# Packed attention and a gated feed-forward block on one core: another table of steps up to the first remainder

## The chip, the cores and the metric

The kernel runs on one core of a Trainium2 chip. Its engines work side by side, each through its own list of instructions in order: TensorE (PE) multiplies, with its weight loads shown apart as PEld; VectorE (DVE) and ScalarE (ACT) do the elementwise work; GpSimd (POOL) helps with a few additions; SyncE (SP) issues the transfers. Where one engine needs what another makes, it waits on a semaphore. The metric is the time of one execution on the device in microseconds (us), as the median of several runs.

## The reference, cut to what matters

```python
def sm_attn(qq, kk, vv):
    s = scale * np.matmul(qq, kk.transpose(0, 1, 3, 2))
    s = s - np.max(s, axis=-1, keepdims=True)
    a = np.exp(s)
    a = a / (np.sum(a, axis=-1, keepdims=True) + 1e-09)
    return np.matmul(a, vv)
p_packed = sm_attn(p, k, v)
out = sm_attn(q, p_packed, p_packed)
...
h = x @ w_in
g = h * (1.0 / (1.0 + np.exp(-h)))
return (g @ w_out).astype(np.float32)
```

There are 8 batches, 8 heads of 64, 576 tokens a batch and 32 packed queries a head; x is the attention's output with the heads side by side (4608 x 512), w_in is 512 x 2048 and w_out 2048 x 512. All inputs are float32.

## The kernel before, in words

The tokens of a batch come in two halves of 288, of which 256 go through the main path; the 32 left over of each half ("rest") are gathered and go through the second product later, four such groups for two batches. The feed-forward block is cut into 16 slices of 128 hidden columns. A unit is one batch and one slice. For each unit PE makes the hidden values (`h_products`, L489: 12 products, 6 a half), ACT takes Silu of them twice, once as float32 and once rounded (`h_values`, L507 to L509), DVE makes the rounding's remainder (`h_lower`, L514), and PE multiplies with the second weight (`out_products`, L521: upper and lower parts, three products for each of four token blocks).

The attention's second half and the first weight are merged: "packs" are the packed values times w_in, four slices at a time (`Packs`: products at L211, split into upper and lower parts at L458 and L461), so that a unit's hidden values are the shares of a token (a2) times a pack.

The weights arrive as 64-bit integers and are turned into float32 on the chip, in 20 chunks: fetched (`wf`, a DMA), scaled by ACT (`ws`, L179 and L180), signed by DVE (`wz`, L184 and L185), joined (`wj`, L191 and L192; for w_out the addition is POOL's), and for w_out split into upper and lower parts (`wu` on ACT, L200, `wl` on DVE, L204). Chunks 0 to 7 are one slice each, even ones of w_in and odd ones of w_out; chunks 8 to 19 are two slices each. Some chunks are staged in a pool of two buffers, some in places of `win` that are not yet in use; a fetch into a place waits until its last chunk is done with.

Up to the first rest group nothing is scheduled by a rule: a table (`ORDER`) names steps one after the other, and each step writes its instructions into the lists of the engines that it uses. So the table sets the order on PE, DVE, ACT and SP at once. In the names, `k`, `q`, `v` load a batch's inputs; `a` and a letter is a step of the attention of batch b: `as` first scores, `ac` their copies, `am` largest, `ax` exponentials, `ar` reciprocals, `at` turned, `ay` spread (16 small DMAs for batches 1 and up, L288), `aa` packed values, `an`, `ai`, `aj` scaled, turned and copied, `aS` second scores, `aC` and `aB` copied and turned to tokens (batch 0 alone), `aT` turned, `aM` less the largest, `aX` exponentials, `aD` shares, `aU` turned back (batch 0 alone), `aH` and `aL` upper and lower part of the shares. `h`, `g`, `l`, `o` and a number are the four steps of a unit, with .0 and .1 where they are done by halves; `pp`, `pu`, `pl` a pack's three; `e` rows of the result; `b` reads partial sums back. `W` and a number is `keep_warm`: as many products of a unit matrix, whose result nobody reads, which keep PE busy.

Units 0 to 3 are batch 0's first slices, 4 to 7 its next; 8 to 15 are batch 1's; 16 to 23 batch 0 again, 24 to 31 batch 1 again; unit 32 is the first rest group. Behind the table a loop runs over the other units and writes the steps of the next batch between them (`step_of`); its first act is `packs_in(2, 1, 2)`, two packs of batch 2.

PE's results go to two pools of two buffers each: `ps_acc` for sums over slices and batch 0's attention, `ps_two` for everything else. A buffer is taken in turn, so a step that takes one waits until the last user but one of that pool has been read. Inputs (`kvq_t`) share two buffers in the same way.

Of the kernel before, what the change touches and what calls it, by code (L numbers as in the profile page):

```python
# [19 lines left out]
P = 128  # L20
# [28 lines left out]


ORDER = """
k0 wf0 ws0 as0.0 as0.1 wf1 am0.0 wf2 am0.1 ax0.0 v0 ax0.1 wz0 W5 at0.0 ay0.0 ar0 W2 wf3 q0 ws2 wj0 ws1 at0.1
W1 wf4 wf5 W5 ay0.1 wz1 aa0 wz2 W2 wj1 an0 ai0 aj0 pp0 aS0.0 ws3 wz3 aS0.1 wu1 wl1 W1 aC0.0 aC0.1 pu0 ws5
aB0.0 wj3 aB0.1 wj2 pl0 aM0.0 wf6 k1 aM0.1 aX0.0 wu3 aD0.0 wf7 W18 ws4 aU0.0 v1 aX0.1 as1.0 aH0.0 aD0.1 W2
aU0.1 wz4 ws6 wl3 ac1.0 as1.1 W5 wj4 ws7 aH0.1 ac1.1 pp1 am1 pu1 wf8 aL0.0 pp2 pl1 pu2 pl2 ax1.0 aL0.1 ax1.1
h0.0 g0.0 at1.0 at1.1 h0.1 wz6 q1 wf9 h1.0 l0.0 wj6 o0.0 g0.1 h1.1 l0.1 wz7 o0.1 ws8 wz5 g1.0 l1.0 pp3 wj5
g1.1 wj7 h2.0 l1.1 pu3 wu5 wz8 ay1 pl3 o1.0 g2.0 wl5 o1.1 wu7 h2.1 ws9 l2.0 wl7 ar1 wf10 wj8 wf11 g2.1 o2.0
h3.0 l2.1 wz9 aa1 g3.0 l3.0 o2.1 ws10 an1 ai1 h3.1 wj9 o3.0 aj1 g3.1 wz10 aS1.0 pp4 aT1.0 aS1.1 pu4 l3.1
wj10 ws11 o3.1 wu10 pl4 h4 g4 aT1.1 h5 aM1.1 wl10 l4 wz11 h6 aM1.0 g5 v2 aX1.1 aX1.0 wj11 o4 l5 g6 h7 aD1.0
o5 wu11 l6 wl11 g7 pp5 o6 aD1.1 k2 pu5 l7 wf12 aH1.0 ws12 wf13 as2.0 aH1.1 aL1.0 o7 pl5 aL1.1 ac2.0 e7.1  # L60
as2.1 ac2.1 am2 ws13 h8 e7.0 g8 h9 l8 g9 h10 pp6 wz12 wz13 ax2.0 l9 o8 ax2.1 wj12 wj13 pu6 wf14 g10 l10 o9
ws14 pl6 h11 at2.0 at2.1 g11 wf15 ar2 ws15 l11 wz14 wj14 o10 h12 g12 wz15 l12 o11 wj15 wu14 h13 o12 g13 wf16
l13 h14 wu15 wl15 ay2 o13 wl14 ws16 g14 h15 wz16 l14 o14 wj16 g15 wf17 l15 ws17 pp7 pu7 wf18 pl7 o15 aa2 h16
e15.0 e15.1 an2 h17 ws18 g16 wz17 wz18 h18 q2 l16 g17 o16 ai2 l17 wj17 aj2 o17 g18 pp8 pu8 aS2.0 wj18 l18
wf19 o18 pl8 h19 b0 aT2.0 ws19 h20 g19 aM2.0 wu18 h21 l19 g20 o19 k3 h22 l20 g21 wl18 wz19 o20 aS2.1 wj19
l21 wu19 g22 o21 aT2.1 l22 wl19 h23 o22 aX2.0 pp10 aD2.0 g23 pp9 pu10 l23 pu9 pl10 o23 pl9 e23.1 h24 h25 g24
e23.0 aH2.0 l24 b1 g25 h26 l25 aM2.1 h27 o24 g26 l26 o25 g27 l27 h28 o26 g28 o27 aX2.1 l28 h29 g29 o28 l29
h30 o29 v3 aD2.1 g30 h31 l30 o30 aH2.1 aL2.1 g31 g32 aL2.0 l31 pp11 l32 pu11 pl11 o31 e31.1 e31.0
"""


# [11 lines left out]
def packed_attention_ffn(ctx: ExitStack, tc: tile.TileContext, pkT, qT, vA, vB, w_in, w_out, out):  # L83
# [13 lines left out]
    nc = tc.nc  # L97
# [29 lines left out]

    def keep_warm(n):

        ps = two_banks()  # L130
        for _ in range(n):
            nc.tensor.matmul(ps[:, 0, :P], ident, ident, start=True, stop=True)
# [83 lines left out]
    class Attention:  # L216
# [80 lines left out]
        def packed(self):  # L297
            v = made["v", self.b]
            self.ps = two_banks()[:, 0] if self.b else sum_banks()[:, 0]
            for par in range(2):  # L300
                for c in range(5):
                    n = min(P, S - c * P)
                    for i in range(NI):
                        h = 2 * i + par
                        if self.b:
                            e = self.e1T[:n, c, i, NP * par : NP * par + NP]
                        else:
                            e = self.e1T[:n, par, c, NP * i : NP * i + NP]
                        nc.tensor.matmul(  # L309
                            self.ps[NP * i : NP * i + NP, par * D : par * D + D],  # L310
                            e,
                            v[:n, c, h * D : h * D + D],
                            start=(c == 0),
                            stop=(c == 4),
                        )
# [258 lines left out]
    def load_parts(b):  # L574
# [171 lines left out]
```

## Time and profile before

| | us |
|---|---|
| median of 3 runs (lowest, highest) | 713.01 (712.46, 713.09) |
| span of the profiled execution, first to last instruction | 711.0 |
| PE busy in it | 692.0 |
| DVE busy | 336.7 |
| ACT busy | 326.7 |
| POOL busy | 18.0 |
| granted clock of PE, mean | 0.996 |
| products of `keep_warm` (L132) | 82 rows, 12.4 us |
| hidden products (L489) | 1536 rows, 454.4 us |
| second products (L521) | 1728 rows, 679.9 us |

Products overlap, so the sums of L489 and L521 are larger than the time that they take together; a row of PE's is not its time from start to start. The timeline lists instructions by start and duration with the idle time before them and what ended it; `x36` behind a row is that many in a run. One product of `keep_warm` makes two rows, and so does each other product of float32. The view by stretches gives the busy time of each engine in a window. The chain of waits goes back from the last instruction to what each one waited for. Line numbers are those of the kernel before; in the changed one all lines from L131 on are one higher.

### The profile page before, as it was taken

How to read it: one execution, taken by the hardware profiler on the slowest of the kernel's cores; microseconds unless marked ns; L12 is line 12 of the kernel's file. 1: busy time of each engine (PE TensorE's matmuls, PEld its weight loads, DVE VectorE, ACT ScalarE, POOL GpSimd, SP SyncE). 2: the span in 40 equal slices, each digit the busy share in tenths (PEclk: the TensorE clock that was granted, in tenths of full speed). 3: DMA queues.
4: the chain of work that ended last, by engine and by line, in shares of the span. 5: the costliest groups of instructions: out<-in, count | busy, mean ns of one | idle time of the engine just before them, and what ended most of it. 6: DMA issues, size and time to landing. Idle time of an engine off the chain costs nothing.

```text
span 711.0 us, 12198 instructions
## 1 busy us (share of the span) xinstructions
PE 692.0 (97%) x5098; PEld 567.0 (80%) x5098; DVE 336.7 (47%) x506; ACT 326.7 (46%) x614; POOL 18.0 (3%) x16
## 2 busy tenths in 40 slices
PE   6789999999999999999999999999999999999997
PEld 4567787878878888888878888878878788888886
DVE  4899997665353336331552315533362333622112
ACT  4577887554434426362532625453352532533221
POOL 0011111110000000000000000000000000000000
PEclk9999999999999999999999999999999999999999
DMA  9858255705012130312111121021301210010002
GB/s 327 322 168 349 76 185 183 265 1 185 1 60 82 33 139 1 111 33 87 67 60 61 39 88 67 27 100 36 137 1 59 83 35 1 1 60 1 0 1 74
DMA packets 31509, 64.15 MB, mean 90 GB/s; under 512 B 19424, under 2 KB 19424, under 8 KB 27104
## 3 DMA queue, kind: packets, MB, share of 16 engines
q1 hardware_dynamic: 31360, 63.26, 25.5%
q8 instruction: 40, 0.66, 0.4%
q10 hardware_dynamic: 96, 0.13, 0.1%
q14 instruction: 13, 0.11, 0.0%
HBM read 47.71 MB, written 11.53 MB: 83 GB/s over the span
## 4 chain that ended last, share of the span: by engine, by line
PE 89%; DVE 6%; DMA 2%; issue 1%; ACT 1%; SPq 0%; DVEq 0%; ACTq 0%
PE ps_acc L521 54%; PE ps_two L489 27%; PE ps_two L211 6%; DMA kvq_t<-in_qT 2%; PE ps_two L309 1%; DVE g_lo L514 1%; DMA kvq_t<-in_pkT 1%; DVE wo_lo L204 1%; DVE win L185 1%; DVE win L191 1%; DVE win L184 0%; DVE win L192 0%; PE ps_acc L211 0%; DVE pw_lo L461 0%; DVE w_raw L184 0%
## 5 line engine op out<-in xcount | busy, mean ns | idle before, releaser
L521 PE MATMUL ps_acc<-wo_hi,g_hi 128*128 128x512 f32 x576 | 229.2, 398 | 0.0
L521 PE MATMUL ps_acc<-wo_lo,g_hi 128*128 128x512 f32 x576 | 225.4, 391 | 0.8 <-DVE wo_lo L204 0.8
L521 PE MATMUL ps_acc<-wo_hi,g_lo 128*128 128x512 f32 x576 | 225.3, 391 | 0.0
L514 DVE TENSOR_TENSOR g_lo<-g,g_hi 128x512 fp32r<-128x512 f32 (+1 forms) x132 | 90.8, 688 | 261.3 <-ACT g_hi L508 261.3
L507 ACT ACTIVATE g<-ps_two 128x512 f32<-128x512 f32 (+1 forms) x132 | 77.5, 587 | 271.2 <-PE ps_two L489 245.6
L489 PE MATMUL ps_two<-a_hi,pw_hi 128*128 128x288 f32 x512 | 152.3, 298 | 2.6 <-DVE pw_lo L461 1.7
L489 PE MATMUL ps_two<-a_lo,pw_hi 128*128 128x288 f32 x512 | 151.5, 296 | 0.0
L489 PE MATMUL ps_two<-a_hi,pw_lo 128*128 128x288 f32 x512 | 150.6, 294 | 0.0
L521 PEld LDWEIGHTS ps_acc<-wo_hi,g_hi 128*128 128x128 f32 x576 | 108.0, 188 | 40.2 <-issue 19.1
L521 PEld LDWEIGHTS ps_acc<-wo_hi,g_lo 128*128 128x128 f32 x576 | 108.1, 188 | 24.4 <-DVE g_lo L514 0.8
L521 PEld LDWEIGHTS ps_acc<-wo_lo,g_hi 128*128 128x128 f32 x576 | 108.2, 188 | 19.6 <-DVE wo_lo L204 1.5
L489 PEld LDWEIGHTS ps_two<-a_hi,pw_hi 128*128 128x128 f32 x512 | 96.4, 188 | 8.1 <-DVE pw_lo L461 2.0
L489 PEld LDWEIGHTS ps_two<-a_lo,pw_hi 128*128 128x128 f32 x512 | 96.1, 188 | 3.5
L489 PEld LDWEIGHTS ps_two<-a_hi,pw_lo 128*128 128x128 f32 x512 | 96.2, 188 | 0.0
L508 ACT ACTIVATE g_hi<-ps_two 128x512 fp32r<-128x512 f32 (+1 forms) x132 | 76.7, 581 | 7.3 <-PE ps_acc L521 7.3
L461 DVE TENSOR_TENSOR pw_lo<-ps_two,pw_hi 128x1024 fp32r<-128x1024 f32 (+1 forms) x35 | 38.3, 1126 | 15.0 <-ACT pw_hi L458 15.0
L458 ACT CAST pw_hi<-ps_two 128x1024 fp32r<-128x1024 f32 (+1 forms) x35 | 31.6, 943 | 21.9 <-PE ps_two L211 21.9
L211 PE MATMUL ps_two<-win,ppT 64*32 64x512 f32 (+1 forms) x560 | 32.5, 560 | 0.4 <-DVE ppT L332 0.4
L509 ACT ACTIVATE rest<-ps_two 128x64 f32<-128x64 f32 (+1 forms) x132 | 30.5, 231 | 0.0
L507 ACT ACT_TABLE_LOAD x15 | 19.2, 1283 | 0.7 <-DVE g_lo L514 0.6
L211 PEld LDWEIGHTS ps_two<-win,ppT 64*32 64x32 f32 x560 | 8.0, 105 | 14.2 <-issue 10.9
L179 ACT ACTIVATE w_raw<-w_raw 128x1024 int32<-128x1024 uint32 (+1 forms) x13 | 13.3, 1021 | 9.5 <-DMA w_raw<-in_w_in 6.2
(101 smaller groups left out, 445.5 us busy)
## 6 DMA issues: line engine op xcount, KB each, us to landing
kvq_t<-in_pkT SPq DMA_DIRECT2D x7, 1216.0 KB, 5.4
kvq_t<-in_vA SPq DMA_DIRECT2D x8, 1024.0 KB, 6.9
out<-o SPq DMA_DIRECT2D x16, 512.0 KB, 2.9
kvq_t<-in_qT SPq DMA_DIRECT2D x7, 1152.0 KB, 5.1
w_raw<-in_w_in SPq DMA_DIRECT2D x6, 1024.0 KB, 8.4
win<-in_w_out SPq DMA_DIRECT2D x3, 1024.0 KB, 6.5
w_raw<-in_w_out SPq DMA_DIRECT2D x3, 1024.0 KB, 4.9
tm<-tm SPq DMA_DIRECT2D x56, 40.0 KB, 2.0
```

What stands on the lines that cost most here:

```text
L179: nc.scalar.activation(low, low.bitcast(U32), AF.Copy, scale=2.0**-29)
L185: nc.vector.scalar_tensor_tensor(low, up, -(2**31), low, op0=ALU.bitwise_and, op1=ALU.bitwise_or)
L191: nc.vector.tensor_scalar(z, up, 3, None, op0=ALU.logical_shift_left)
L211: nc.tensor.matmul(bank(par)[NP * i : NP * i + NP], lhs(r, i), rhs(r, i), start=True, stop=True)
L458: nc.scalar.copy(self.hi, self.ps[:, :, : self.nf * P])
L461: nc.vector.tensor_tensor(self.lo, self.ps[:, :, : self.nf * P], self.hi.bitcast(F32), ALU.subtract)
L489: nc.tensor.matmul(bank, p[:, par, cols], a[:, par], start=(n == 0), stop=(n == len(todo) - 1))
L507: nc.scalar.activation(g, ps[..., :MAIN], AF.Silu)
L508: nc.scalar.activation(g_hi, ps[..., :MAIN], AF.Silu)
L509: nc.scalar.activation(to, ps[..., MAIN:HS], AF.Silu)
L514: nc.vector.tensor_tensor(g_lo[:, c], g[:, c], g_hi[:, c].bitcast(F32), ALU.subtract)
L521: nc.tensor.matmul(bank, g[:, rows], w[:, f], start=(first and n == 0), stop=(last and n == 2))
```

## The change

The table of steps is another one, with the same steps except for the `W`s: 69 products of them, in 8 places, instead of 41 in 9. `keep_warm` now holds one tile for as long as no other step takes a buffer of `ps_two`, instead of taking one at each call. Nothing behind the table is changed.

```diff
 ORDER = """
-k0 wf0 ws0 as0.0 as0.1 wf1 am0.0 wf2 am0.1 ax0.0 v0 ax0.1 wz0 W5 at0.0 ay0.0 ar0 W2 wf3 q0 ws2 wj0 ws1 at0.1
+W8 wf0 wf1 ws0 wz0 wj0 ws1 k0 as0.0 wz1 wj1 W2 as0.1 am0.0 am0.1 wf2 wu1 wl1 ax0.0 W10 at0.0 v0 wf3 ay0.0 ax0.1 q0
...
     def two_banks():
 
+        made.pop("warm", None)
         return ps_two.tile([P, 2, 512], F32, name="ps_two")
...
     def keep_warm(n):
 
-        ps = two_banks()
+        if "warm" not in made:
+            made["warm"] = two_banks()
         for _ in range(n):
-            nc.tensor.matmul(ps[:, 0, :P], ident, ident, start=True, stop=True)
+            nc.tensor.matmul(made["warm"][:, 0, :P], ident, ident, start=True, stop=True)
```

On PE, around the second half of batch 0's attention, the list was this. L211 into `ps_acc` are the second scores (`aS0`), L359 the turns to tokens (`aB0`), L132 the fillers, L379 and L381 the turns back (`aU0`):

```order
L211 MATMUL ps_acc<-kvq_t,ppT 32x288 x16
L132 MATMUL ps_two<-ident 128x128
L359 MATMUL ps_acc<-ident,tm 128x128 x10
L132 MATMUL ps_two<-ident 128x128 x18
L379 MATMUL ps_acc<-ident,tm 128x128 x2
L381 MATMUL ps_acc<-ident,tm 128x32
```

Now the same place on PE reads:

```order
L212 MATMUL ps_acc<-kvq_t,ppT 32x288 x8
L133 MATMUL ps_two<-ident 128x128 x4
L360 MATMUL ps_acc<-ident,tm 128x128 x10
L133 MATMUL ps_two<-ident 128x128 x36
L380 MATMUL ps_acc<-ident,tm 128x128 x2
L382 MATMUL ps_acc<-ident,tm 128x32
```

A pack (`pp1`) has moved in between the two halves of the second scores (the row shown is the second half), and the fillers ahead of the turns back are 36 instead of 18.

On ACT, where the first Silu of the kernel stands (a2_hi is batch 0's `aH0`; L257 are the exponentials of batch 1, `ax1`), the list was:

```order
L430 CAST a2_hi_414<-ps_acc_381 128x576
L458 CAST pw_hi_288<-ps_two_418 128x2x128
L458 CAST pw_hi_288<-ps_two_435 128x2x128
L257 ACTIVATE tm_447,den_448<-tm_393,nm_428 128x576 x2
L507 ACT_TABLE_LOAD
L507 ACTIVATE g_461<-ps_two_452 128x256
```

The same place on ACT now:

```order
L431 CAST a2_hi_449<-ps_acc_423 128x576
L508 ACT_TABLE_LOAD
L508 ACTIVATE g_463<-ps_two_454 128x256
L509 ACTIVATE g_hi_461<-ps_two_454 128x256
L510 ACTIVATE rest_93<-ps_two_454 128x32
L201 CAST wo_hi_91<-win_90 128x512
L508 ACTIVATE g_463<-ps_two_468 128x256
L509 ACTIVATE g_hi_461<-ps_two_468 128x256
L510 ACTIVATE rest_93<-ps_two_468 128x32
L258 ACT_TABLE_LOAD
L258 ACTIVATE tm_482,den_483<-tm_438,nm_479 128x576 x2
L508 ACT_TABLE_LOAD
```

The exponentials of batch 1 have moved behind `g0.0` and `g0.1`, and a table load stands on each side of them. The two halves of `aX1` have moved apart in the same way, so there are 34 table loads in the whole program where there were 30.

At the end of the table, on DVE, L564 adds `e31`'s partial sums (o), L514 from `rest_93` is `l32`, and L461 are the lower parts of packs: the first is `pl11`, the next two those of `packs_in(2, 1, 2)`. Before:

```order
L514 TENSOR_TENSOR g_lo_2017<-g_2018,g_hi_2016 128x512
L514 TENSOR_TENSOR g_lo_2023<-rest_93,g_hi_2022 128x512
L461 TENSOR_TENSOR pw_lo_2038<-ps_two_2027,pw_hi_2037 128x1024
L564 TENSOR_TENSOR o_1791<-ps_acc_1836,o_1791 128x1024
L564 TENSOR_TENSOR o_1789<-ps_acc_1829,o_1789 128x1024
L461 TENSOR_TENSOR pw_lo_2083<-ps_two_2064,pw_hi_2082 128x1024
L461 TENSOR_TENSOR pw_lo_2087<-ps_two_2073,pw_hi_2086 128x1024
```

And now, on DVE:

```order
L435 TENSOR_TENSOR a2_lo_2052<-tm_1747,a2_hi_2051 128x576
L565 TENSOR_TENSOR o_1880<-ps_acc_1822,o_1880 128x1024
L515 TENSOR_TENSOR g_lo_2037<-rest_93,g_hi_2036 128x512
L565 TENSOR_TENSOR o_1882<-ps_acc_1829,o_1882 128x1024
L462 TENSOR_TENSOR pw_lo_2072<-ps_two_2055,pw_hi_2071 128x1024
L462 TENSOR_TENSOR pw_lo_2104<-ps_two_2085,pw_hi_2103 128x1024
L462 TENSOR_TENSOR pw_lo_2108<-ps_two_2094,pw_hi_2107 128x1024
```

`pl11` has moved behind both additions. On PE its products (`pp11`) stood ahead of unit 31's second products (`o31`) and now stand behind them, directly ahead of the two packs:

```order
L522 MATMUL ps_acc_1829<-wo_lo_92,g_hi_2029 128x512
L522 MATMUL ps_acc_1829<-wo_hi_91,g_lo_2030 128x512
L212 MATMUL ps_two_2055<-win_90,ppT_1720 32x512 x8
L212 MATMUL ps_two_2085<-win_90,ppT_1720 32x512 x8
L212 MATMUL ps_two_2094<-win_90,ppT_1720 32x512 x8
L522 MATMUL ps_acc_2111<-wo_hi_91,g_hi_2036 128x512
```

Other moves that the prediction speaks of: `k0` stands behind `wf0` and `wf1` on SP instead of ahead of them; on DVE `am1`, `wz4`, `wj4` and `pl2` stand behind `aL0.1` instead of ahead of it, and `wz5` and `wj5` ahead of it instead of behind; on SP `wf10` stands ahead of `q1` and of the 16 spreads of `ay1` instead of behind them; `at2.1` stands behind `g20` instead of with `at2.0` near `h11`; `k3` and `v3` stand at the table's end.

More of the change, by code (lines that the diff above doesn't have):

```diff
@@ L51 @@
 ORDER = """
-k0 wf0 ws0 as0.0 as0.1 wf1 am0.0 wf2 am0.1 ax0.0 v0 ax0.1 wz0 W5 at0.0 ay0.0 ar0 W2 wf3 q0 ws2 wj0 ws1 at0.1
[L53 to L66, printed above, removed]
@@ L67 @@
-e23.0 aH2.0 l24 b1 g25 h26 l25 aM2.1 h27 o24 g26 l26 o25 g27 l27 h28 o26 g28 o27 aX2.1 l28 h29 g29 o28 l29
-h30 o29 v3 aD2.1 g30 h31 l30 o30 aH2.1 aL2.1 g31 g32 aL2.0 l31 pp11 l32 pu11 pl11 o31 e31.1 e31.0
+W8 wf0 wf1 ws0 wz0 wj0 ws1 k0 as0.0 wz1 wj1 W2 as0.1 am0.0 am0.1 wf2 wu1 wl1 ax0.0 W10 at0.0 v0 wf3 ay0.0 ax0.1 q0
+ws2 at0.1 wz2 wf4 wf5 ay0.1 ar0 wj2 wf6 W5 aa0 an0 W2 ai0 aj0 W2 pp0 aS0.0 pp1 ws3 wz3 wj3 pu0 pu1 pl0 aS0.1 aC0.0
+aC0.1 pl1 W4 aB0.0 wu3 aB0.1 wl3 aM0.0 ws5 aX0.0 ws6 aM0.1 aX0.1 ws4 aD0.0 W36 aU0.0 aD0.1 wz5 k1 wj5 aH0.0 aL0.0
@@ new lines @@
+as1.0 aU0.1 wf7 wf8 ws7 v1 ac1.0 as1.1 aH0.1 ac1.1 aL0.1 h0.0 g0.0 wu5 h0.1 g0.1 am1 ax1.0 h1.0 l0.0 o0.0 wz4 l0.1
+h1.1 ax1.1 g1.0 g1.1 wz6 o0.1 wj4 pp2 at1.0 wl5 at1.1 l1.0 o1.0 wz7 pu2 pl2 h2.0 l1.1 wf9 wf10 ws9 wj6 g2.0 h2.1
+g2.1 wz9 pp3 pu3 pl3 l2.1 l2.0 q1 ws8 o1.1 h3.0 h3.1 wj7 wj9 wu7 wl7 g3.0 l3.0 ar1 o2.0 o2.1 o3.0 wz8 wj8 ws10 g3.1
+ay1 aa1 l3.1 an1 ai1 pp4 pu4 wz10 wf11 ws11 o3.1 aj1 wj10 aS1.0 pl4 h4 aT1.0 wf12 h5 wu10 g4 aM1.0 wl10 ws12 l4
+aS1.1 aT1.1 g5 o4 h6 h7 wz11 wj11 l5 o5 aX1.0 aD1.0 g6 wu11 l6 k2 as2.0 aH1.0 g7 wl11 wf13 wf14 aM1.1 l7 aL1.0 aX1.1
@@ new lines @@
+aD1.1 o6 ac2.0 pp5 pu5 pl5 pp6 aH1.1 aL1.1 o7 pu6 pl6 h8 g8 wz12 h9 l8 h10 e7.0 g9 e7.1 o8 l9 ws13 wz13 g10 h11 ws14
+h12 l10 wj13 wj12 o9 o10 g11 l11 wf15 g12 pp7 as2.1 wz14 wj14 pu7 pl7 l12 o11 ac2.1 ws15 wz15 h13 h14 wf16 ws16 wj15
+g13 o12 h15 am2 l13 wu15 wl15 g14 l14 ax2.0 h16 wf17 wz16 o13 ax2.1 o14 g15 l15 wu14 wl14 ws17 wj16 wf18 g16 l16
+wz17 h17 wj17 o15 e15.0 at2.0 e15.1 b0 g17 l17 h18 ws18 wz18 wj18 h19 o16 o17 g18 l18 g19 l19 pp8 pu8 pp10 pl8 o18
+wu18 pu10 pl10 wf19 h20 g20 at2.1 l20 ar2 h21 ws19 wl18 o19 h22 q2 v2 g21 h23 l21 wz19 wj19 wu19 o20 o21 g22 ay2 l22
@@ L69 @@
+g23 wl19 aa2 an2 pp9 ai2 o22 l23 pu9 pl9 aj2 aS2.1 aT2.1 aM2.1 aS2.0 aX2.1 aT2.0 aM2.0 o23 e23.1 h24 g24 h25 e23.0
+l24 g25 l25 h26 o24 g26 h27 h28 o25 b1 l26 o26 aX2.0 g27 l27 aD2.0 g28 h29 h30 aD2.1 aH2.1 o27 l28 aL2.1 o28 g29 l29
+g30 h31 o29 l30 o30 g31 l31 g32 o31 aH2.0 aL2.0 pp11 e31.0 l32 k3 e31.1 pu11 pl11 v3
 """
```

## The prediction

> **What bounds it.** I read the page first, then the chain of waits, then the busy time by stretch, then the timeline of the first 90 us.
>
> ```profile
> span 711.0 us, 12198 instructions
> PE 692.0 (97%) x5098; PEld 567.0 (80%) x5098; DVE 336.7 (47%) x506; ACT 326.7 (46%) x614; POOL 18.0 (3%) x16
> ```
>
> PE is busy for 692 of 711 us, so a new order of the same work can only move the 19 us in which PE stands still, and the time in which it runs fillers. The chain, followed through the first 82 us, shows where PE stops waiting.
>
> ```profile
> 7.92 12.26 DMA kvq_t<-in_qT
> ...
> 75.58 1.15 DVE wo_lo L204
> 76.73 0.04 issue
> 76.77 2.79 PE ps_acc L521 x11
> ```
>
> The last wait is for `wl11` (L204) at 76.73; from there on the chain is PE alone. What the table does before that point moves the end one for one; a wait that it makes behind it is added in full.
>
> ```profile
> 20.00:25.00 5.00, 4.78 (x40) 3.81 (x41) 2.87 (x4) 2.14 (x4) 0.41 (x1) 0.67 1.02 417
> ...
> 35.00:40.00 5.00, 2.39 (x40) 1.85 (x22) 4.93 (x10) 4.48 (x12) 0.00 (x0) 1.00 0.97 395
> ...
> 75.00:80.00 5.00, 4.71 (x45) 2.50 (x44) 4.86 (x10) 4.32 (x7) 0.00 (x0) 1.00 0.00 0
> 80.00:90.00 10.00, 10.00 (x89) 7.54 (x82) 9.12 (x13) 8.12 (x13) 0.00 (x0) 1.00 0.49 168
> ```
>
> Columns: stretch, length, busy PE, PEld, DVE, ACT, POOL, granted clock, DMA share, GB/s. From 35 to 80 DVE is busy for 4.9 of every 5 us (first and last of nine such rows): it is the bound there, and PE from 80 on. So I follow DVE up to the first point where both orders have done the same DVE work for it, `h8`, and then look for new PE waits behind it.
>
> **The front, up to batch 0's split.**
>
> ```profile
> 17.36 0.72 PE L211 MATMUL ps_acc<-kvq_t,ppT 64*32 64x288 f32 x16
> 20.22 1.21 PE L211 MATMUL ps_acc<-kvq_t,ppT 64*32 64x288 f32 x16 [2.15 <-DMA kvq_t<-in_qT]
> 23.48 0.96 DVE L388 TENSOR_REDUCE on_tokens<-ps_acc 128x24 f32<-128x768 f32 x1 [0.56 <-PE ps_acc L359]
> 23.73 4.18 PE L132 MATMUL ps_two<-ident 128*128 128x128 f32 x36
> 28.20 0.96 DVE L412 TENSOR_TENSOR tm<-tm,on_tokens 128x768 f32<-128x768 f32 x1
> 29.30 0.41 PE L379 MATMUL ps_acc<-ident,tm 128*128 128x128 f32 x2 [1.39 <-DVE tm L412]
> 31.96 0.68 DVE L204 TENSOR_TENSOR wo_lo<-w_raw,wo_hi 128x512 fp32r<-128x512 f32 x1
> ```
>
> `k0` now stands behind two weight loads, which makes the first scores about 3 us late (1 MB at some 370 GB/s). The second half of q hides that: the same bytes (k, v, four weight chunks) are queued ahead of it in both orders, so it still lands near 20.2, and `aS0.1` waits for it. `aM0.0` (L388) began at 23.48; I take 23.3, because PE stays warm over the fillers (0.72 instead of 1.21 us for those scores) but `wl3` (0.68) now stands ahead of it on DVE and itself waits for ACT's `wu3`. Bounds: 22.6, with no such wait, and 24.4, where the ten fillers ahead of `at0.0` run slow.
>
> Then `W36`. `W18` left 36 rows in 4.18 us, 0.116 each; `W36` is 72 rows, 8.4 us. The chain that it covers, from `aM0.0` to the end of `aD0.0` (28.20 + 0.96), is 5.7 us. The filler ends 2.6 us behind the work it waits for: `aU0.0` starts at 31.6, not 29.1.
>
> ```profile
> 30.47 0.64 ACT L430 CAST a_hi<-ps_acc 128x576 fp32r<-128x576 f32 x1 [1.90 <-PE ps_acc L381]
> ...
> 33.05 0.69 ACT L179 ACTIVATE win<-win 128x512 int32<-128x512 uint32 x1
> ...
> 34.48 1.35 DVE L247 TENSOR_REDUCE mx<-tm 128x2 f32<-128x1152 f32 x1
> ...
> 37.08 0.40 PE L489 MATMUL ps_two<-a_hi,pw_hi 128*128 128x288 f32 x1 [1.74 <-DVE pw_lo L461]
> ...
> 37.28 0.74 DVE L434 TENSOR_TENSOR a_lo<-ps_acc,a_hi 128x576 fp32r<-128x576 f32 x1
> ...
> 37.78 1.28 ACT L507 ACT_TABLE_LOAD   x1
> 39.08 0.38 ACT L507 ACTIVATE g<-ps_two 128x256 f32<-128x256 f32 x1
> ...
> 79.50 0.72 PE L211 MATMUL ps_two<-kvq_t 64*32 64x288 f32 x16
> ```
>
> From 31.6 on PE: `aU0.0` 1.1 us (29.30 until `aH0.0` could start at 30.47), `as1.0` 0.7 (like the row at 79.50), `aU0.1` 1.1, `as1.1` 0.7, to 35.2. On ACT `aH0.0` ends at 33.4, then `ws7` (two instructions like L179's, 1.3) and `ac1.0` (0.64) to 35.4, `aH0.1` to 36.0; DVE's `aL0.1` (0.74) ends at 36.8. `h0.0` needs the bank that `ac1.0` frees: 35.4 against 37.08, 1.7 us earlier; the split is complete at 36.8 against 38.02 (37.28 + 0.74), 1.2 earlier. That is the gain; without the overhang of W36 it would be 2.6 us larger.
>
> **What DVE owes for it.**
>
> ```profile
> 40.66 0.42 DVE L191 TENSOR_SCALAR win<-win 128x512 int32<-128x512 int32 x1
> 41.11 0.69 DVE L192 CUSTOM_DVE_ANT_0 win<-win 128x1024 uint16<-128x1024 uint16 x1
> ...
> 42.06 0.42 DVE L184 TENSOR_SCALAR win<-win 128x512 f32<-128x512 f32 x1
> 42.51 0.69 DVE L185 SCALAR_TENSOR_TENSOR win<-win 128x512 int32<-128x512 int32 x1
> ...
> 81.79 0.74 DVE L434 TENSOR_TENSOR a_lo<-tm,a_hi 128x576 fp32r<-128x576 f32 x1
> ...
> 83.75 0.40 PE L489 MATMUL ps_two<-a_hi,pw_hi 128*128 128x288 f32 x1
> ```
>
> Moved behind the split: `am1` (1.35 + 0.17), `wz4`, `wj4` (about 1.05 each, by the two pairs above) and `pl2` (0.36), 4.0 us; moved ahead of it: `wz5` and half of `wj5`, 1.4. So 2.6 us more DVE work lies between `aL0.1` and `aL1.1`, where before took 82.53 - 38.02 = 44.5 us.
>
> Two waits are new there. On ACT the exponentials of batch 1 now stand between two Silu groups: two extra table loads of 1.28 us, and two more at `aX1.1`. `g1.0` then ends near 44.5, when DVE has been ready for 0.45 us (and PE for 2.3, which DVE's lag covers). The ACTIVATE at 39.08 follows its load at once. [...]
>
> The second wait is SP's.
>
> ```profile
> 39.43 11.23 SPq L288 DMA_DIRECT2D tm<-tm  x16
> ...
> 52.43 1.73 PE L309 MATMUL ps_two<-kvq_t,tm 128*32 128x64 f32 x80
> ```
>
> `wf10` writes over win 8 to 11, so it waits for `wl5` (now at 43.5), and `q1` and the 16 spreads of `ay1` queue behind it: they start at 44.5 instead of 39.43. With the same 13.0 us, `aa1` comes at 57.5; PE would be there at 56, and behind `aa1` DVE's `an1` loses 0.7 us.
>
> Sum: 36.8 + 44.5 + 2.6 + 0.45 + 0.7 = 85.05 for `h8`, against 83.75. By then the new order has done 0.55 us more PE work (`pp6`, 0.98, but not `as2.1`, 0.4): net **+0.8 us**. Lowest end: the 2.6 us and both waits vanish in idle time that DVE had before, -1.7 (the split's lead and the 0.55); highest: slow fillers and late weights, +3.
>
> **Behind it.** The table's end:
>
> ```profile
> 194.87 1.09 PE L211 MATMUL ps_two<-win,ppT 64*32 64x512 f32 x16
> ...
> 196.06 1.02 ACT L458 CAST pw_hi<-ps_two 128x1024 fp32r<-128x1024 f32 x1 [0.64 <-PE ps_two L211]
> ...
> 197.11 1.22 DVE L461 TENSOR_TENSOR pw_lo<-ps_two,pw_hi 128x1024 fp32r<-128x1024 f32 x1 [0.96 <-ACT pw_hi L458]
> ...
> 198.85 1.95 PE L211 MATMUL ps_two<-win,ppT 64*32 64x512 f32 x32
> ```
>
> `pp11` stood ahead of `o31`; now it stands behind it, directly ahead of the two packs that `packs_in(2, 1, 2)` adds (the last row is both of them). `ps_two` has two buffers, so the second of those packs takes pp11's and waits for `pl11`. From the start of `pp11` to the end of `pl11` before took 198.33 - 194.87 = 3.46 us; PE has 1.95 us of work meanwhile (the last row). All of PE queues behind it: **+1.5 us**. DVE does `e31.1` in between, which ends before `pu11` does. Bounds 1.0 to 2.2.
>
> ```profile
> 99.88 1.60 PE ps_two L489 x12
> 101.47 2.73 PE ps_acc L521 x12
> ```
>
> `ay2` now follows `at2.1` closely: some 13 us of DMA, as for `ay1`, against `h21` to `h23` and `o19` to `o21` on PE (3 x 1.60 + 3 x 2.73 = 13.0): **+0.3** (0 to 0.8).
>
> At nothing I cost: the later `k3` and `v3` (`k3` goes out near 201, behind `e31.0`'s row on SP, and is read only after the four rest units and two units of batch 2, 4 x 2.73 and more on PE; a read that came sooner would be late by what is left of a load); the second pair of table loads (ACT idles 1.9 of 10 us even from 80 to 90; uncovered, 2.6 us); POOL's joins, which move with `wj` and run beside DVE; and the one tile that all fillers now share, which spares them waits for a buffer, below 0.2 us each, in time that PE fills anyway.
>
> 0.8 + 1.5 + 0.3 = 2.6: span 713.6. The profiled span lies 2.0 below the median of the three runs, 713.0, so **715.6**.
>
> **Rivals.** One: the lead carries (27%). If DVE's extra 2.6 us disappear in waits that it had before, `h8` comes with the split's lead: -1.2 - 0.55 = -1.7, and with the 1.5 and 0.3 behind it 713.1; if the front is also at its early bound (0.7 less), `ay2` costs nothing and the table's end 1.0, 711.6; if the 0.1 us in which DVE idles in each 5 us goes too, 0.8 in all, 710.8. It decides where PE's waits up to 76 us stop being DVE's. For it: PE gets its first product 1.7 us sooner, and the clock of 0.67 from 20 to 25 us should go. [...] Against it: 4.9 of 5 us DVE.
>
> ```profile
> win<-in_w_out SPq DMA_DIRECT2D x3, 1024.0 KB, 6.5
> ```
>
> Two: fillers and weights (20%). [...]
>
> [...]
>
> **Numbers.** The sum above has 53%, its own range 713.6 to 717.5. The range for 8 in 10 is 711.5 to 718.8. A change under 0.2%, 1.4 us, cannot be told from none. Faster (below 711.6): 0.12, from the first rival's lowest end; within: 0.26 (0.15 of the first rival, 0.11 of the sum's low end); slower (above 714.4): 0.62.
>
> **What would show it.** `aU0.0` starting right as W36 ends, with DVE's `aD0.0` done 2 to 3 us earlier; first product near 35.4; `h8` near 85; a PE gap of 1.5 us ahead of the second pack of `packs_in(2, 1, 2)`. Wrong if the last DVE wait of PE comes before 76 us, or if that gap is missing.

## The result, and the profile after

| | before | changed |
|---|---|---|
| median, us (lowest, highest of 4) | 712.74 (711.62, 713.09) | 721.40 (720.42, 722.10) |
| ratio to before, 95% interval | | 1.0129 [1.0107, 1.0150] |
| profiled execution: time, span | 713.01, 711.0 | 721.24, 719.5 |
| `h8` starts | 83.82 | 89.98 |
| first product of unit 32 (`o32`) | 200.80 | 209.45 |

The change makes the kernel 1.3% slower. The forecast had the sign but 715.6 us: a loss of 2.6 where there are 8.5. The page of the changed kernel:

```profile
span 719.5 us, 12299 instructions
PE 701.0 (97%) x5154; PEld 576.6 (80%) x5154; DVE 334.3 (46%) x506; ACT 331.5 (46%) x618; POOL 17.3 (2%) x16
```

PE is busy for 9 us more. The fillers make 138 rows and 20.5 us instead of 82 and 12.4, and rows take longer where the clock is low: a row of L522 takes 0.63 us at 66 us, with 0.70 granted, and 0.39 at 56, with 1.00. The marks of the table place the loss. 6.2 us are there at `h8`, 2.5 more come between it and `o32`, and behind the table nothing is added. The chain of waits up to `h8` (start, duration, what), answering the one that ended in `wl11` at 76.73:

```profile
44.05 0.58 DVE wo_lo L205
44.63 0.02 SPq L174
...
45.11 7.73 DMA kvq_t<-in_qT
52.84 0.02 issue
52.86 0.59 SPq L289
...
58.15 1.93 DMA tm<-tm
60.07 0.14 issue
60.21 2.13 PE ps_two L310 x74
...
63.25 1.89 PE ps_two L212 x16
65.14 2.86 PE ps_acc L522 x6
```

It runs through DVE to `wl5`, on through SP's `wf10`, `q1` and `ay1` (L289), and from `aa1` (L310) on it is PE alone. SP itself stands still in the middle of the spreads: eight have gone out by 50.33 and the ninth follows at 52.86, as `q1` lands. SP's waits from 30 to 62 us say so (who, for what: us in total, times, longest):

```profile
SPq L289 <- DMA kvq_t<-in_qT: 2.5, 1, 2.5
```

Why the ninth spread stands behind that landing was not followed. The stretches, in the columns of before:

```profile
20.00:25.00 5.00, 3.71 (x75) 2.78 (x60) 2.24 (x5) 2.82 (x6) 1.04 (x1) 1.00 1.01 414
...
35.00:40.00 5.00, 4.64 (x40) 3.20 (x39) 3.95 (x7) 4.97 (x11) 0.36 (x1) 1.00 0.00 2
...
50.00:55.00 5.00, 5.00 (x28) 4.41 (x27) 4.96 (x9) 3.90 (x8) 1.42 (x1) 1.00 0.62 172
55.00:60.00 5.00, 2.29 (x14) 1.41 (x12) 4.44 (x8) 2.24 (x5) 0.00 (x0) 1.00 0.27 56
60.00:65.00 5.00, 4.29 (x91) 1.94 (x91) 2.60 (x5) 0.00 (x0) 0.00 (x0) 0.62 1.01 395
65.00:70.00 5.00, 5.00 (x40) 3.43 (x33) 2.73 (x5) 4.12 (x4) 1.89 (x1) 0.70 0.99 416
```

PE stands still from 57.0 to 60.2, but for 0.3 us at 57.5, and then its clock is granted at 0.62 and 0.70; ACT and DVE run dry behind it, with 0.00 and 2.60 of 5 us from 60 to 65. From 35 to 40 the transfers move 2 GB/s, while `q1`, whose buffer is free by 36.6, waits on SP behind `wf10`. Behind `h8` the chain shows PE waiting for a table load of ACT (L508 is the first Silu):

```profile
89.98 1.61 PE ps_two L490 x12
...
91.66 1.28 ACT L508
...
94.17 0.04 issue
94.21 1.86 PE ps_two L490 x12
```

`h9` takes 1.6 of the time between, so 1.0 us is lost; the same stands at 170.60 for `g24`. And the front, on PE's timeline (start, duration, line, shape, count; in brackets the idle time before and what ended it):

```profile
11.03 3.62 PE L133 MATMUL ps_two<-ident 128*128 128x128 f32 x20
14.49 1.25 PE L277 MATMUL ps_acc<-ident,tm 128*128 128x128 f32 x10
...
20.38 0.40 PE L212 MATMUL ps_two<-win,ppT 64*32 64x128 f32 x9
22.07 0.31 PE L212 MATMUL ps_two<-win,ppT 64*32 64x128 f32 x4 [1.29 <-issue]
...
24.99 8.20 PE L133 MATMUL ps_two<-ident 128*128 128x128 f32 x72
33.03 0.38 PE L380 MATMUL ps_acc<-ident,tm 128*128 128x128 f32 x2
```

### The profile page after: what moved, and what is told of

Read it like the earlier page. It is cut to its first block, busy times and chain, and to the rows that moved or that the text cites. A ratio compares the mean times of both kernels' runs of the same rounds, so it can differ in the third digit from the quotient of the medians.

```text
span 719.5 us, 12299 instructions
## 1 busy us (share of the span) xinstructions
PE 701.0 (97%) x5154; PEld 576.6 (80%) x5154; DVE 334.3 (46%) x506; ACT 331.5 (46%) x618; POOL 17.3 (2%) x16
## 4 chain that ended last, share of the span: by engine, by line
PE 94%; DMA 2%; DVE 1%; ACT 1%; SPq 1%; issue 0%; ACTq 0%
PE ps_acc L522 55%; PE ps_two L490 27%; PE ps_two L212 7%; PE ps_two L133 2%; PE ps_two L310 2%; DMA kvq_t<-in_qT 1%; DMA kvq_t<-in_pkT 1%; SPq L289 1%; PE ps_acc L212 0%; ACT L508 0%; DMA tm<-tm 0%; PE ps_acc L310 0%; DVE win L186 0%; PE ps_acc L380 0%; DVE mx L248 0%
## 5 line engine op out<-in xcount | busy, mean ns | idle before, releaser
L522 PE MATMUL ps_acc<-wo_hi,g_hi 128*128 128x512 f32 x576 | 229.5, 398 | 0.0
L522 PE MATMUL ps_acc<-wo_lo,g_hi 128*128 128x512 f32 x576 | 225.8, 392 | 0.0
L522 PE MATMUL ps_acc<-wo_hi,g_lo 128*128 128x512 f32 x576 | 225.4, 391 | 0.0
L515 DVE TENSOR_TENSOR g_lo<-g,g_hi 128x512 fp32r<-128x512 f32 (+1 forms) x132 | 89.2, 676 | 268.4 <-ACT g_hi L509 268.4
L508 ACT ACTIVATE g<-ps_two 128x512 f32<-128x512 f32 (+1 forms) x132 | 77.5, 587 | 254.3 <-PE ps_two L490 234.9
L522 PEld LDWEIGHTS ps_acc<-wo_hi,g_hi 128*128 128x128 f32 x576 | 108.4, 188 | 40.1 <-issue 19.8
L522 PEld LDWEIGHTS ps_acc<-wo_hi,g_lo 128*128 128x128 f32 x576 | 108.4, 188 | 23.7
L522 PEld LDWEIGHTS ps_acc<-wo_lo,g_hi 128*128 128x128 f32 x576 | 108.4, 188 | 18.5
L212 PE MATMUL ps_two<-win,ppT 64*32 64x512 f32 (+1 forms) x560 | 34.0, 573 | 4.5 <-DVE pw_lo L462 1.6
L133 PEld LDWEIGHTS ps_two<-ident 128*128 128x128 f32 x138 | 19.2, 223 | 3.8 <-issue 2.3
```

The costliest lines, as they stand in the source:

```text
L133: nc.tensor.matmul(made["warm"][:, 0, :P], ident, ident, start=True, stop=True)
L212: nc.tensor.matmul(bank(par)[NP * i : NP * i + NP], lhs(r, i), rhs(r, i), start=True, stop=True)
L508: nc.scalar.activation(g, ps[..., :MAIN], AF.Silu)
L515: nc.vector.tensor_tensor(g_lo[:, c], g[:, c], g_hi[:, c].bitcast(F32), ALU.subtract)
L522: nc.tensor.matmul(bank, g[:, rows], w[:, f], start=(first and n == 0), stop=(last and n == 2))
```

## The experiments

Theory: the spreads of `ay1` run beside `q1`'s 1.15 MB, end late, and PE's pause costs its clock too; behind `h8` the table loads and `pp11` are added. The rivals: DVE's order decides anyway; fillers and front decide.

### a1_q1: q1 ahead of wf10

```diff
-... l1.1 wf9 wf10 ws9 ... l2.0 q1 ws8 ...
+... l1.1 wf9 q1 wf10 ws9 ... l2.0 ws8 ...
```

> The changed kernel with one step moved: q1 ahead of wf10 on SP, so that q's 1.15 MB go out as soon as their buffer is free (about 37 us, when the transfers stand still) and not at 45.11, just ahead of the 16 spreads of ay1. Theory queue (the spreads are slow because q1's bytes are ahead of them): the spreads take the 13.0 us that they took in the kernel before, from 45.6, so aa1 comes at 58.5 instead of 60.21; PE then idles 1.8 us ahead of it instead of 3.5, and with that short a pause the granted clock of 0.62 and 0.70 from 60 to 70 us should be gone (2.3 us); span 719.5 less 1.7 to 4.0, so 715.5 to 717.8. Rival order (aa1 is late only because at1.1 ends late on DVE, and the spreads take what they take): aa1 stays at 60, span within 0.5 of 719.5.

Ratio to before 1.0084 [1.0058, 1.0110], profiled span 713.9. On the timelines of SP and PE:

```profile
35.47 0.33 SPq L146 DMA_DIRECT2D kvq_t<-in_qT  x1
43.55 0.33 SPq L174 DMA_DIRECT2D win<-in_w_out  x1
44.25 11.28 SPq L289 DMA_DIRECT2D tm<-tm  x16
```

```profile
56.99 1.68 PE L310 MATMUL ps_two<-kvq_t,tm 128*32 128x64 f32 x74 [1.09 <-DMA tm<-tm]
```

The spreads take 12.7 us from their start to `aa1` instead of 14.6, PE waits 1.1 us, and the clock is 1.00 from 55 to 70. The split was 1.1 us sooner in this execution for another reason (below); from the split to the end of `aL1.1` it takes 46.95 us against 51.5 in the changed kernel. So `q1`'s place costs 4.5 us: theory queue. By the medians it is 3.2 (0.45%). The later runs repeat it: the same stretch takes 46.4 to 46.95 us in all five with `q1` moved in this way (a1_q1 and the four c runs), and 50.4 to 52.6 in the six others that leave the changed kernel's order there (a4_w18, a5_pp11, a7_k0, d1_load, d2_load, e1_32b).

### a2_queue: ay1 ahead of wf10 too

```diff
-... l1.1 wf9 wf10 ws9 ... l2.0 q1 ws8 ... g3.1 ay1 aa1 ...
+... l1.1 wf9 q1 ay1 wf10 ws9 ... l2.0 ws8 ... g3.1 aa1 ...
```

> The changed kernel with q1 and all of ay1 ahead of wf10 on SP, as in the kernel before. Theory queue as in the run above, with the 1 MB of wf10 out of the way of the spreads too: they start at 45.3, right behind at1.1 on DVE (44.54 + 0.77), and end as fast as before: aa1 at 58.3; half clock gone; span 715.5 to 717.5. If only q1's bytes mattered this gives the same as the run above; if wf10's mattered, aa1 comes a microsecond or more sooner than there. wf10 then leaves SP near 57 and lands near 62, and ws10 on ACT wants it near 54.4: rival late weight, o4 waits for wl10, which eats up to 3 us of the gain.

Ratio 1.0175 [1.0149, 1.0200]: slower still. The chain, then PE's timeline:

```profile
57.58 4.82 DMA win<-in_w_out
62.40 0.02 issue
62.42 1.10 ACT win L180
63.52 0.99 ACT win L181
64.50 0.27 ACT g L508
```

```profile
65.85 0.44 PE L329 MATMUL ps_two<-ident,pp 128*128 128x128 f32 x1 [5.25 <-DVE pp L320]
```

The late weight was the right rival with the wrong price. `ws10` stands ahead of part of `g3.1` on ACT, DVE's `l3.1` waits for that, and `an1` stands behind `l3.1`: PE loses 5.25 us, not 3. `wf10`'s place ahead of the spreads protects this; of the two places only `q1`'s cost time.

### a3_exps: batch 1's exponentials ahead of the first Silu

```diff
-... aH0.1 ac1.1 aL0.1 h0.0 g0.0 wu5 h0.1 g0.1 am1 ax1.0 ... ax1.1 ... at1.0 wl5 at1.1 ...
+... aH0.1 ac1.1 am1 ax1.0 aL0.1 ax1.1 h0.0 g0.0 at1.0 at1.1 wu5 h0.1 g0.1 ... wl5 ...
```

(on top of a2_queue)

> As the run above, and batch 1's am1, ax1 and at1 stand ahead of the first Silu again, as in the kernel before, so two table loads of 1.28 us go, and at1.1 ends on DVE near 41 instead of 45.3. Theory order: the spreads then run from 41 to 54, aa1 waits for PE alone (PE is there at 56.7 or sooner), no half clock, and PE waits only for DVE: span 719.5 less 3.5 (the wait) less 2.3 (the half clock), 713 to 715. Rival debt (DVE's 2.6 us of work moved behind the split decides, whatever the spreads do): span 715.5 to 717, with DVE busy for 4.9 of 5 us up to 75 and PE waiting for it in several places.

Ratio 1.0115 [1.0091, 1.0139], span 717.4. The stretches:

```profile
35.00:40.00 5.00, 3.12 (x28) 2.24 (x19) 3.08 (x5) 2.86 (x8) 0.00 (x0) 0.86 0.66 234
40.00:45.00 5.00, 3.45 (x12) 2.81 (x12) 4.40 (x9) 3.82 (x11) 0.00 (x0) 0.50 0.15 33
```

`am1` now delays `aL0.1`, PE waits 1.86 us for it and 1.55 for the first Silu, and a clock of 0.50 follows from 40 to 45. The spreads, done early, no longer matter (`aa1` waits for no transfer), and the total is near the changed kernel's: neither expectation held whole. It is 0.6% faster than a2_queue, on which it is built, and slower than a1_q1, which leaves the Silu first. What the order of the exponentials costs by itself was not run alone.

### a4_w18, and the fillers again in c2_w26

```diff
-... aD0.0 W36 aU0.0 ...
+... aD0.0 W18 aU0.0 ...
```

> The changed kernel with 18 fillers instead of 36 ahead of aU0.0. Theory overhang: aU0.0 starts when aD0.0 is done, near 30.9 instead of 33.03; DVE's pauses of 0.60 and 1.02 us at 34.8 and 36.6 go, and the split is complete 1.6 to 2.0 us sooner (36.2 instead of 38.04); at1.1, ay1 and aa1 follow, span 717.5 to 718. Rival cold: PE now pauses 2 us from 29 to 31, the products behind run at half clock, and the split comes no sooner: span 719 to 720.5.

Ratio 1.0120 [1.0094, 1.0145], not to be told from the changed kernel's; span 717.4.

```profile
30.07 0.41 PE L380 MATMUL ps_acc<-ident,tm 128*128 128x128 f32 x2 [1.85 <-DVE tm L413]
```

`aU0.0` starts as DVE is done, and the split is complete at 36.01, 2.0 us sooner, of which 0.95 is a sooner front. That is theory overhang. But PE has paused 1.85 us, its clock is 0.73 and 0.58 from 30 to 40, as rival cold has it, and `aa1` again waits 2.36 us behind `q1`. So the number in between was tried, with the repairs told below.

### a5_pp11 and b1_pp11: the table's end, undone and alone

```diff
-... l31 g32 o31 aH2.0 aL2.0 pp11 e31.0 l32 k3 e31.1 pu11 pl11 v3
+... l31 g32 pp11 aH2.0 aL2.0 pu11 pl11 o31 e31.0 l32 k3 e31.1 v3
```

> The changed kernel with pp11, pu11 and pl11 ahead of o31 again. Theory buffer (the second pack of packs_in(2, 1, 2) waits for pl11): the wait of 1.58 us near 208 goes, nothing else changes, span 719.5 less 1.6, 717.9. Rival moved wait (PE then waits for pl11 or l31 somewhere else, because DVE's additions of e31 are in the way): a wait of about 1 us appears within 10 us of it, span 719 to 719.5.

Ratio 1.0118 [1.0078, 1.0158], span 718.3; PE is busy for all of 200 to 220, and the list of PE's waits has no `pw_lo` any more: theory buffer. The ratio alone would not show it. In the kernel before:

```diff
-... l31 pp11 l32 pu11 pl11 o31 e31.1 e31.0
+... l31 l32 o31 pp11 e31.1 e31.0 pu11 pl11
```

> The kernel before with one part of the change alone: pp11, pu11 and pl11 behind o31 and the additions of e31, as in the changed kernel. Theory buffer: PE's second pack of packs_in(2, 1, 2) waits 1.5 to 1.6 us for pl11, span 711.0 plus 1.5, ratio 1.002. Rival: DVE is ahead here and the additions end sooner, so the wait is under 0.5 us and the time does not move.

Ratio 1.0010 [0.9996, 1.0023]. The time does not settle 1.5 us; PE's waits (engine, line, releaser: us, times, longest) do:

```profile
PE ps_two L211 <- DVE pw_lo L461: 1.7, 1, 1.7
```

### a6_tables: the halves of the exponentials together

```diff
-... l5 o5 aX1.0 aD1.0 ... wf14 aM1.1 l7 aL1.0 aX1.1 ... aS2.0 aX2.1 aT2.0 ... o26 aX2.0 ...
+... l5 aM1.1 o5 aX1.0 aX1.1 aD1.0 ... wf14 l7 aL1.0 ... aS2.0 aT2.0 ... o26 aX2.1 aX2.0 ...
```

> The changed kernel with the two halves of aX1, and of aX2, next to each other again (aM1.1 and aX1.1 moved up to aX1.0, aX2.1 moved down to aX2.0), so two pairs of table loads go, 34 to 30 in the program. Theory table load (the first Silu behind the exponentials puts its load of 1.28 us behind the wait for h8, or h24, and PE, which has two banks, stands still for 1.0 us): the waits at 93.2 to 94.21 and at 172.1 to 173.15 go, span 719.5 less 2.0, 717.5. Rival banks (PE would wait there anyway, because g8 and g24 take 1.2 us and only two banks are there): the waits shrink to some 0.2 us or stay, span 718.5 to 719.5.

Ratio 1.0132 [1.0105, 1.0159]: nothing gained. Both waits are gone, but `aM1.1` now stands ahead of `aD1.0` and `wl11` on DVE, and `aX1.1` ahead of `g6` on ACT. PE waits 0.89 us for `g6`'s bank, 0.32 for `wo_hi`, and then as below; its clock is 0.83 in the stretch from 80 to 90.

```profile
85.26 0.79 PE L522 MATMUL ps_acc<-wo_lo,g_hi 128*128 128x512 f32 x1 [0.76 <-DVE wo_lo L205]
```

### a7_k0: k0 first

```diff
-W8 wf0 wf1 ws0 wz0 wj0 ws1 k0 as0.0 ...
+W8 k0 wf0 wf1 ws0 wz0 wj0 ws1 as0.0 ...
```

> The changed kernel with k0 ahead of wf0 and wf1 on SP, as in the kernel before. PE's first scores then start near 4.4 instead of 7.60. Theory front: the second scores' gap of 1.29 us (20.78 to 22.07) is the landing of q0's second half, which then leaves SP 3 us sooner, so the gap goes, aM0.0 comes at 23.0 or sooner instead of 25.22, and the end moves by what of this reaches aa1 and lasts, 1.5 to 2.2 us: span 717.3 to 718. Rival instructions: q0 had landed at 18.0 (issued 11.6, 6.4 us to landing), and the gap is one in which PE gets no instructions, at the same place of its list in all runs (behind row 9 of pp1): then a gap of 1.3 to 1.6 us stays behind row 9 of pp1 although everything ahead of it is earlier, and aM0.0 gains only what k0 brings past v0's landing, 0 to 2 us.

Ratio 1.0163 [1.0133, 1.0194], a miss by both:

```profile
15.89 2.39 PE L277 MATMUL ps_acc<-ident,tm 128*128 128x128 f32 x10 [5.38 <-ACT tm L258]
```

The table has `ws0` and `ws1` ahead of the first exponentials on ACT, so these now wait for the weights. `k0`'s place is part of the new order, not a fault of it. The gap behind row 9 of `pp1` is absent here, with PE idle for 5.4 us shortly before.

### d1_load and e1_32b: a small Silu, and 32 bytes

```diff
+    silu = const.tile([P, 8], F32, name="silu")
...
+        "T": lambda n: nc.scalar.activation(silu, ident[:, :8], AF.Silu),
...
-... aX1.1 aD1.1 ... aX2.1 aT2.0 ...
+... aX1.1 T0 aD1.1 ... aX2.1 T0 aT2.0 ...
```

> The changed kernel with one small Silu more (128x8, its result is read by nobody) on ACT right behind aX1.1 and another right behind aX2.1, with every step in its place. Theory table load: the loads of 1.28 us then run in ACT's pause behind the exponentials instead of behind the wait for h8 and h24; the waits of 1.0 us at 93.2 and 172.1 go, and nothing on DVE moves: span 719.5 less 2.0, 717.5. Rival order (what moving aX1.1 up cost was due to the loads themselves, which now only hit something else): a wait of a microsecond shows between 82 and 94, span 718.5 or more.

Ratio 1.0220 [1.0199, 1.0241], span 726.9: 7.4 us longer, although both waits are gone and only one of 0.9 us, for `ay2`, is new. Of the 7.4 us, 2.6 are a late front in this execution (the split is complete at 40.60 instead of 38.04), but the second products had also become slower everywhere, 2.79 to 2.80 us a unit in the chain for 2.73. To part the Silu from its tile:

```diff
+    spare = const.tile([P, 8], F32, name="spare")
+    nc.gpsimd.memset(spare, 0.0)
```

> The changed kernel with one unused tile of 32 bytes per partition more in the pool of constants, set to zero by POOL at the start; all pools behind it move by 32 bytes. Theory place (the second products are slower where their operands start at such a place): each unit's second products take 2.79 instead of 2.73 us in the chain, 144 units of them 8 us, span 727 to 728 with the waits of the changed kernel in place. Rival Silu (the slower products of d1_load come from the Silus or from the chip): span 719.5, 2.73 us.

Ratio 1.0235 [1.0215, 1.0256], with the waits of the changed kernel. Its chain (lines are three higher), and its groups of instructions (the last numbers are busy us, and mean ns of one):

```profile
224.48 1.59 PE ps_two L493 x12
226.07 2.80 PE ps_acc L525 x12
```

```profile
L525 PE MATMUL ps_acc<-wo_hi,g_hi 128*128 128x512 f32 x576 | 232.2, 403 | 0.0
```

The same group without the tile, in the changed kernel:

```profile
L522 PE MATMUL ps_acc<-wo_hi,g_hi 128*128 128x512 f32 x576 | 229.5, 398 | 0.0
```

A unit's second products take 2.79 to 2.80 us in the chain where they took 2.73, its hidden products 1.59 for 1.60. 144 units by 0.06 are 8.6 us; the ratios differ by 1.06%, 7.5 us, and the span of 725.7 lies below the 727 that was expected. Theory place: less the 2.0 us of table loads and with the 0.9 for `ay2`, 7.5 make 6.4 us for d1_load, whose ratio lies 0.91%, 6.5 us, above the changed kernel's. All five runs with the 32 bytes show 2.79 to 2.80, and d2_load and c4_best, which have the small Silus without them, 2.73 and 2.74.

### d2_load: the Silu without a tile

```diff
+        "T": lambda n: nc.scalar.activation(rest[:, NF - 1, 1, 0, :8], ident[:, :8], AF.Silu),
```

> The changed kernel with the two small Silus behind aX1.1 and aX2.1, written into a part of an existing tile that a later Silu overwrites, so that no tile moves. Theory table load: the waits near 93 and 172 go, second products stay at 2.73 us: span 719.5 less 2.0, 717.5. Rival: PE waits there for something else, span 719 or more.

Ratio 1.0111 [1.0093, 1.0130], span 716.6. The chain has the three hidden products in one piece:

```profile
89.76 4.80 PE ps_two L490 x36
94.55 2.74 PE ps_acc L522 x12
```

The load now runs at 83.63, ahead of the wait for `h8`, and `g8` starts as soon as `h8` is there; for `h24` the load runs at 167.26. Each wait was the table load: 1.0 us. It is not quite free: ACT's copy `ac2.0` stands behind it, and PE waits 0.34 us for that copy at 85.72. Of the span's 2.9 us, 2.0 are the two waits and 0.2 are there at `h8`; the other 0.7 were not followed. The intervals of this run and of the changed kernel overlap, so PE's waits carry this and not the time.

### c1_three, c2_w26, c3_w4, c4_best: the repairs together

The first is a1_q1, a5_pp11 and d1_load in one; each of the next two has one line more. All three have the 32 bytes, which the fourth has not.

```diff
-... aD0.0 W36 aU0.0 ...
+... aD0.0 W26 aU0.0 ...
```

```diff
-... ax0.0 W10 at0.0 ...
+... ax0.0 W4 at0.0 ...
```

> Three repairs of the changed kernel at once: q1 ahead of wf10, pp11 with pu11 and pl11 ahead of o31, and the two small Silus behind aX1.1 and aX2.1. If the three terms are apart from each other they add up: 713.9 (the run with q1 moved alone) less 1.6 less 2.0, 710.3, within 1 us of the kernel before. If q1's gain was partly a lucky front in the one profiled execution (its first second-half scores came 1.1 us sooner than in the changed kernel), 711.5 to 712.5.

> As the run above, with 26 fillers instead of 36 ahead of aU0.0: 5.9 us, as long as the chain that they cover. Theory overhang: aU0.0 starts as aD0.0 ends, 2.1 us sooner, PE stays at full clock (with 18 it fell to 0.58 from 35 to 40), and the split comes 1.6 to 2 us sooner; span 1.6 below the run above, 708.5 to 710. Rival DVE (behind the split DVE is the bound, and the lead dies there as in the rival of my prediction it should not): span within 0.5 of the run above.

> As the run above, with 4 fillers instead of 10 ahead of at0.0. In the changed kernel these ran from 11.03 to 14.65 at the slow rate, while ax0.0 was done at 13.0. Theory overhang again: at0.0 starts near 13.0, 1.5 us sooner than in the changed kernel; span 0.5 to 1.2 below the run above. On the gap of 1.3 to 1.6 us behind row 9 of pp1: if PE lacks instructions there, the gap moves by the 12 rows left out, to behind row 5 of the second scores' second half; if it is a landing of data for those scores, it stays ahead of them.

> All repairs without a new tile: q1 ahead of wf10, 26 fillers ahead of aU0.0 and 4 ahead of at0.0, pp11 ahead of o31, small Silus. The run with the same table but the 32 bytes (c3_w4) had a span of 714.0 with second products of 2.79 us; 144 units less 0.06 us each is 8 us less. Theory place and terms that add up: span 705 to 707, ratio to the kernel before 0.990 to 0.995, faster than both kernels. If the 32 bytes were not the reason: span 713 to 715, ratio 1.005.

| | ratio to before, 95% interval | span |
|---|---|---|
| d1_load (32 bytes, Silus) | 1.0220 [1.0199, 1.0241] | 726.9 |
| c1_three (and q1, pp11) | 1.0115 [1.0095, 1.0135] | 718.5 |
| c2_w26 (and 26 fillers) | 1.0079 [1.0061, 1.0098] | 718.0 |
| c3_w4 (and 4 fillers) | 1.0054 [1.0040, 1.0067] | 714.0 |
| c4_best (without the 32 bytes) | 0.9970 [0.9958, 0.9983] | 706.8 |

c1_three missed its number by the 32 bytes, which were not known then; against d1_load, with the same bytes, `q1` and `pp11` bring 1.05% by the medians, 7.5 us, where the profiles gave 4.5 and 1.6 apart; the rest was not followed. The two lines of fillers bring 0.36% and 0.25%; the intervals of c1_three and c3_w4 do not overlap. In c2_w26's profiled execution the front was 2.0 us later than in c1_three, so its split came no sooner (38.10 for 38.12), and the span missed what was expected; c3_w4 gained 4.0 us of span where 0.5 to 1.2 were expected, for its split came at 34.09. c4_best, 709.62 us by the median, is 0.3% faster than the kernel before and faster than the changed one. Its span lies where it was expected, its ratio does not reach 0.995. Against c3_w4, which has the 32 bytes, it is 7.2 us of span less for 8 expected. Its chain at `h8`:

```profile
78.35 2.96 PE ps_acc L522 x12
81.31 4.80 PE ps_two L490 x36
```

2.5 us ahead of the kernel before; the clock is 1.00 in each stretch from 20 to 100 us. In c3_w4 (lines one higher) the gap of the front has moved:

```profile
20.46 0.70 PE L213 MATMUL ps_acc<-kvq_t,ppT 64*32 64x288 f32 x11 [0.72 <-issue]
```

It stood behind row 9 of `pp1`'s 16; with 12 rows fewer ahead of it, it stands behind row 5 of the second scores, 12 rows on.

## Why the prediction was wrong

**The front** failed: `aM0.0` at 25.22, past the upper bound of 24.4. The step was "it still lands near 20.2, and `aS0.1` waits for it". The half of q left SP 3.7 us later than before, but landed sooner, 6.4 us behind its issue at the most, where it had taken 12.26 in the kernel before (the view of L146, up to 23 us):

```profile
DMA to landing us min/median/max: 5.3/5.8/6.4
```

Issued by 12.04, it was there by 18.4; what it shared the queues with was not followed. Instead PE lost 1.29 us in the gap of the front, and about 1.1 to slow fillers: the 20 rows ahead of `at0.0` took 3.62 us, where a1_q1 had 2.50 and c2_w26 3.88 with the same list ahead of them, so this part differs from one execution to the next. That bound I had, with its price, but only as a corner; the gap I did not have.

**W36** was right: 8.20 us for 8.4, and `aU0.0` starts 2.1 us behind `aD0.0` (30.89) for 2.6. With the front's delay the lead was gone: the split was complete at 38.04, the kernel before had 38.02.

**DVE's debt** was right: from the split to the end of `aL1.1` 46.95 us in a1_q1 and 46.4 in c4_best, where the terms without the spreads made 47.55. But the sum held only for as long as DVE was the bound, and in the changed kernel it was not: from 60 to 70 us DVE is busy for 2.60 and 2.73 of 5, and PE's last wait for it ahead of `h8` ends at 62.80 (0.51 us). That is the sign of being wrong that the prediction named, a last wait before 76 us. **The table loads at `g1.0`** cost DVE nothing, for 0.45, and PE 1.57, for the 2.3 that I took as covered.

**The spreads** had the place right and the size wrong, and this is the largest miss: 0.7 us, "With the same 13.0 us, `aa1` comes at 57.5", where a1_q1 puts 4.5 on `q1`'s place. They took 14.6, from 45.58. The 13.0 came from a row in which q was already landing; here `q1` left SP just ahead of them, though I had written that they queue up together. And the sum priced a wait, not what comes behind it: `aa1`, `pp4` and `o3.1` at a clock of 0.62 and 0.70, and dry queues on DVE and ACT. Counted from the split, `h8` came 3.7 us later than by all my terms. The prediction had a low clock behind a wait, 0.67 from 20 to 25 us with a wait of 2.15 up to 20.22, and did not ask it of this one.

**The second pair of table loads** was the second mistaken step: "At nothing I cost ... (ACT idles 1.9 of 10 us even from 80 to 90)". That idle time lies ahead of `h8`, while the load stood behind the wait for it: 1.0 us, and 1.0 for `g24`, which I had not looked at.

**The table's end** was right, 1.58 for 1.5. **`ay2`** cost nothing, inside its bounds. Of the **rivals**, the first fell with the front. The second, fillers and weights, stands behind the +3 at `h8` and the upper end of the range: no run shows slow fillers in `W36`, whose 72 rows took 8.20 us in every timeline that has them. The low clock came from 60 to 70 us instead, 0.62 and 0.70, and a late weight in a2_queue, where PE lost 5.25 us.

Together at `h8`: 1.2 from the split and 3.7 behind it, nearly all of it the spreads, which cost 3.8 more than their price. Behind it: 2.0 from table loads, 0.1 from `pp11`, less 0.3 for `ay2`; the remaining 0.8 of the other sign lies in how units follow each other and was not followed.

## What to carry to other kernels

A load whose buffer is free should not queue behind one that still waits, least of all just ahead of many small transfers that are waited for: here that place of `q1` cost 4.5 us. A wait of PE is priced with the work behind it: here 2.4 us of waiting, and then 10 us at a clock of 0.62 and 0.70. Idle time of an engine covers an instruction only if the instruction can start in it, and here a table load of 1.28 us, behind 2.26 us in which ACT stood idle, cost PE 1.0: ask what the instruction stands behind, not how idle its engine is on average.

## What the runs showed of the hardware

**Where operands lie.** 32 bytes per partition more ahead of the later pools made the second products 2.2% slower (2.79 for 2.73 us a unit) in all five runs that had them, and the hidden products not at all (1.59 for 1.60). Which operand it is was not tried. A tile added for an experiment needs this control.

**A gap of PE in the front.** It is 1.28 to 2.00 us long and stands behind row 9 of `pp1` in the changed kernel and in eleven of the twelve runs with the same list of PE up to there; in c4_best and c3_w4, which have 12 rows fewer ahead of it, it is 0.71 and 0.72 us long and stands 12 rows later. It has no releaser in the profile, and it was absent in the twelfth, a7_k0, where PE had paused for 5.38 us before it; the transfer engines were full at the time (1.01 in the changed kernel from 20 to 25 us). That PE gets no instructions there, the rival of a7_k0, is not shown: the one transfer on an instruction queue near the gap is at 19 to 20 us in the changed kernel, ahead of the gap, and none falls into it.

**The clock.** A pause of PE of 2.4 us (the changed kernel, up to 60.21) was followed by two stretches of 5 us at 0.62 and 0.70, one of 2.15 (the kernel before, up to 20.22) by 0.67, one of 1.85 (a4_w18, up to 30.07) by 0.73 and 0.58. The length alone does not decide: one of 1.74 (the kernel before, up to 37.08) was followed by 1.00, one of 1.68 (b1_pp11, up to 19.84) by 0.66. Nor does the column tell everything: in the changed kernel the first scores at 7.60 take 1.21 us, where 16 rows of the same shape take 0.70 at 19.90, and the clock reads 1.00 at both.
